# Sums and products with v in four groups of 32 TensorE columns, in a softcapped attention with a gated feed-forward layer

## The chip, the cores and the metric

The kernel runs on one core of one Trainium2 chip. The metric is the device time of one execution in microseconds (us); lower is better. Before the change the median of three runs is 743.75 us (742.98 to 746.29).

## The reference

```python
def _attn_ref(q, k, v, cap):                      # each 8 x 12 x 448 x 64, cap = 30
    scores = scale * np.matmul(q, k.transpose(0, 1, 3, 2))
    scores = cap * np.tanh(scores / cap)
    scores = scores - np.max(scores, axis=-1, keepdims=True)
    attn = np.exp(scores)
    attn = attn / (np.sum(attn, axis=-1, keepdims=True) + 1e-09)
    return np.matmul(attn, v)

def _moe_ref(x, w_val, conv_w, w_out):            # x: 8 x 448 x 768
    ...                                           # gate_pre: causal convolution of x, 5 taps a channel
    gate = 1.0 / (1.0 + np.exp(-gate_pre))
    val = x @ w_val
    return gate * val @ w_out
```

Attention runs over 8 batches and 12 heads; the heads' outputs, side by side, are the x of the second function. All is float32.

## The kernel before, in words

Heads are taken in pairs, six pairs to a batch, 48 pairs in all (`p` from 0 to 47). A tile of 128 partitions holds the 64 dimensions of both heads, one below the other. No maximum is subtracted before the exponent; a small term, `guard`, is added to each sum.

The steps of one pair:

- `load_q`, `load_k`, `load_v` (SyncE's queue, SP) fetch the inputs; `tq`, `tk` (line 305) transpose q and k in blocks of 32 on VectorE (DVE).
- `scores` (L326, TensorE, PE): for each of four groups of 112 keys, both heads at once, keys on partitions and 448 queries along the columns. From pair 13 on (`NPLAIN`) q and k are split in a high and a low part and each product is three matmuls; before that, it is one float32 matmul, which PE makes in two passes.
- `tanh` (L334) and `exp` (L338) on ScalarE (ACT).
- `add` (L345, L348) on DVE: the four groups of keys are added, so that the sums need fewer matmuls: pairs 0 to 5 don't add (four sums steps), pairs 6 to 10 add in twos (two steps), from pair 11 on all four are added (one step).
- `attnv` ("products with v", L363, PE): for each group of keys and each head `j` one matmul with v (112 x 64) as the weights; head 0 writes partitions 0 to 63 of the PSUM tile `psa` (or `psf`), head 1 the partitions 64 to 127. In PE's array these are two groups of 64 columns.
- `sums` (L375, PE): the same with a tile of ones as the weights, so that all 64 partitions of a head hold the sum of each query, in `psz`.
- `turn_sums` (L383, DVE) transposes blocks of 32 x 32 into `zt`: after it, queries lie on partitions. `norm_recip` adds `guard` on the first column of each of the 14 blocks (L389) and takes the reciprocal of these 128 x 14 numbers in one instruction (L390). `spread` (L396) transposes them back, each repeated 32 times. `norm_mul` (L404) multiplies `psa` by the result: `u`, the attention's output.
- `x_hi` (L409, ACT) and `x_lo` (L240, DVE) split u; `conv` (L421, L423, L425) computes the five taps on DVE.

A batch then has the feed-forward part: `sigmoid` (L431, ACT), `val` (L446 to L448, PE, three matmuls for high and low parts), `gate` (L452, DVE), `gated_hi` (L455, ACT), `gated_lo` (L240, DVE), `out_part` (L475 to L477, PE), `store` (L483, ACT) and the output's DMA (L487). The weights are brought from float64 words to two float32r parts in twelve steps during the first dozen pairs (L140 to L150, ACT and DVE).

The order on all engines is written out by hand: each step has a time in units of pairs (`STEADY`, `EARLY`, `PAIRED`, `TOGETHER` and others), all steps are sorted by it, and each engine executes its own in that order, each waiting for what it needs. So a late step holds back what stands behind it on its engine. The tiles `zt` and `rc` exist once.

Of the kernel before, what the change touches and what calls it, by code (L numbers as in the profile page):

```python
# [7 lines left out]
F32 = mybir.dt.float32  # L8
# [5 lines left out]
ALU = mybir.AluOpType  # L14
# [7 lines left out]
P = 128  # L22
ENG = mybir.EngineType

CH = 112
LOAD_ROWS = 112

BLK = 32
# [173 lines left out]
def fast_path(tc, io, u2, q, k, v, w_val, conv_w, w_out, out, capt):  # L202
# [5 lines left out]
    nc = tc.nc  # L208
    B, H, S, D = q.shape
# [4 lines left out]
    NKT = S // CH  # L214
# [6 lines left out]
    PAD = KW - 1  # L221
    GW = TL + S
    ROWS = [slice(j * D, (j + 1) * D) for j in range(2)]

    with ExitStack() as ctx:
        cpool = ctx.enter_context(tc.tile_pool(name="cpool", bufs=1))
        wk = ctx.enter_context(tc.tile_pool(name="wk", bufs=2))
# [18 lines left out]
        guard = cpool.tile([P, 1], F32, name="guard")  # L246
        nc.vector.scalar_tensor_tensor(guard, capt, -1.0, capt, ALU.mult, ALU.min)
        nc.scalar.activation(guard, guard, AF.Exp)
        nc.vector.tensor_scalar_mul(guard, guard, EPS)  # L249
        ones = cpool.tile([P, D], F32, name="ones")  # L250
        nc.gpsimd.memset(ones, 1.0)
        cw = cpool.tile([P, NCC, KW], F32, name="cw")

# [42 lines left out]
        loads, vloads = {(name, 0): t[:, PAD:] for name, t in zip("qk", u2)}, {}  # L296
# [21 lines left out]
        def scores(p, i):  # L318
# [5 lines left out]
            for n, (x, y) in enumerate(parts):  # L324
                for j, r in enumerate(ROWS):
                    nc.tensor.matmul(  # L326
# [23 lines left out]
        def bank(p, name):  # L350

            if p < NEARLY and p % 2:
                return ps_f.tile([P, 512], F32, name="psf")
            return ps_a.tile([P, 512], F32, name=name)

        def attnv(p, i):

            st = state[p]
            if i == 0:
                st["o"] = bank(p, "psa")  # L360
            t = st["p", i]
            for j, r in enumerate(ROWS):
                nc.tensor.matmul(  # L363
                    st["o"][r, :S], vloads[p][:, j, i], t[:, j], start=(i == 0), stop=(i == NKT - 1)
                )

        def sums(p, i):

            st = state[p]
            n = len(tables[p]["sums"])  # L370
            if i == 0:
                st["z"] = bank(p, "psz")
            t = st["p" if n == NKT else "a", i]
            for j, r in enumerate(ROWS):
                nc.tensor.matmul(st["z"][r, :S], ones[:CH], t[:, j], start=(i == 0), stop=(i == n - 1))  # L375
            if i == n - 1:
                vloads.pop(p)

        def turn_sums(p):

            st = state[p]
            st["zt"] = wk.tile([P, S], F32, name="zt", bufs=1)
            nc.vector.transpose(st["zt"], st.pop("z")[:, :S])  # L383

        def norm_recip(p):
            st = state[p]
            rc = wk.tile([P, S // BLK], F32, name="rc", bufs=1)
            col = st["zt"].rearrange("p (c e) -> p c e", e=BLK)[:, :, 0]
            nc.vector.tensor_scalar(rc, col, guard, None, ALU.add)  # L389
            nc.vector.reciprocal(rc, rc)  # L390
            st["rc"] = rc

        def spread(p):
# [116 lines left out]
        def at(when, f, *a):  # L510
# [7 lines left out]
            q_hi=lambda p: half_hi("q", p), k_hi=lambda p: half_hi("k", p),  # L518
            q_lo=lambda p: half_lo("q", p), k_lo=lambda p: half_lo("k", p),
            scores=scores, tanh=tanh, exp=exp, add=add, av=attnv, sums=sums, turn_sums=turn_sums, recip=norm_recip,  # L520
            spread=spread, mul=norm_mul, x_hi=x_hi, x_lo=x_lo, conv=conv,
        )
        for p, table in enumerate(tables):
            for name, f in steps.items():
                x = table.get(name, ())
# [165 lines left out]
def kernel(tc, q, k, v, cap, w_val, conv_w, w_out, out):  # L691
    nc = tc.nc
    with tc.tile_pool(name="cap_pool", bufs=1) as pool, tc.tile_pool(name="io", bufs=2) as io:
        capt = pool.tile([P, 1], F32, name="capt")
        nc.sync.dma_start(capt, cap.rearrange("(o c) -> o c", o=1).partition_broadcast(P))

        pad = conv_w.shape[0] - 1
        u2 = [pool.tile([P, pad + q.shape[2]], F32, name=f"u{i}") for i in range(2)]
        for t, src in zip(u2, (q, k)):
            load_blocks(nc, t[:, pad:], src, 0)  # L700
        mag = pool.tile([1, 1], F32, name="mag")
        nc.vector.scalar_tensor_tensor(mag, capt[0:1], -1.0, capt[0:1], ALU.mult, ALU.max)
        small = pool.tile([1, 1], I32, name="small")
        nc.vector.tensor_scalar(small, mag, CAP_FAST, None, ALU.is_le)
        flag = nc.values_load(small, min_val=0, max_val=1)
        with tc.If(flag != 0) as cmp:
            fast_path(tc, io, u2, q, k, v, w_val, conv_w, w_out, out, capt)
        with cmp.Else():
            general_path(tc, q, k, v, w_val, conv_w, w_out, out, capt)
# [30 lines left out]
```

## Time and profile before

| | |
|---|---|
| median of three runs | 743.75 us (742.98, 743.75, 746.29) |
| profiled execution | span 739.6 us from its first to its last instruction; no other time of it is given |
| PE busy | 717.1 us, 97% |
| DVE busy | 593.0 us, 80% |
| ACT busy | 534.7 us, 72% |
| matmul passes of the products (L363) | 768 |
| matmul passes of the sums (L375) | 284 |
| L383, transpose of the sums | 48 times, 31 us |
| L389 and L390, guard and reciprocal | 48 times each, 11.3 and 11.6 us |
| mean granted TensorE clock | 0.998 |

Rows of the profile name the line, the engine, the operation, the tiles (output <- inputs), the shape, and the count (x); behind the bar stand busy time in us, mean duration of one in ns, and the idle time of the engine just before, with what ended it. In a timeline a row begins with its start and its duration in us, rows of equal kind are merged, and the idle time before it stands in brackets. Rows of a stage have start:end and length, the busy time of PE, PEld (weight loads), DVE, ACT and POOL, the granted clock, and the share of the DMA engines with GB/s. Rows of waits say who waited for whom: us in total, times, and the longest. PEldq is PE's sequencer. Matmul passes overlap, so their durations add up to more than the time they take.

### The profile page before, as it was taken

The numbers are of one execution on the slowest core, as the hardware profiler recorded it, in microseconds if no ns is written. First come the engines' busy times: TensorE is split into PE (matmuls) and PEld (weight loads), VectorE is DVE, ScalarE is ACT, GpSimd is POOL, SyncE is SP. The second block draws the span as 40 slices with busy tenths as digits, with TensorE's granted clock in tenths as the row PEclk, the third lists the DMA queues.
The fourth block names the chain that finished last, engine by engine and source line by source line (L and its number), as shares of the span: only waits on it lengthen the run. The fifth ranks groups of instructions, "written<-read, shape, count | busy, mean of one in ns | idle before, by whom it ended". The sixth has DMA issues, their size and how long they took to land.

```text
span 739.6 us, 10858 instructions
## 1 busy us (share of the span) xinstructions
PE 717.1 (97%) x3972; PEld 488.8 (66%) x3972; DVE 593.0 (80%) x972; ACT 534.7 (72%) x708; POOL 9.0 (1%) x16
## 2 busy tenths in 40 slices
PE   5999999999999999999999999999999999999997
PEld 2333655556767776686677766757766876676997
DVE  2899999888997789988899669988899778997410
ACT  5899977787876678776957679587787659774311
POOL 0000001000000000000000000000000000000000
PEclk9999999999999999999999999999999999999999
DMA  6998867854223332224331333223322333200001
GB/s 109 223 212 209 202 171 154 225 118 80 39 49 80 74 74 38 61 67 88 57 57 47 88 75 65 39 69 74 73 38 61 70 87 57 51 24 33 23 22 68
DMA packets 241820, 63.75 MB, mean 86 GB/s; under 512 B 228448, under 2 KB 235616, under 8 KB 241760
## 3 DMA queue, kind: packets, MB, share of 16 engines
q1 hardware_dynamic: 241760, 62.98, 38.6%
q8 instruction: 33, 0.54, 0.3%
q14 instruction: 27, 0.22, 0.1%
HBM read 51.94 MB, written 11.01 MB: 85 GB/s over the span
## 4 chain that ended last, share of the span: by engine, by line
PE 52%; DVE 21%; ACT 13%; issue 2%; SPq 1%; DMA 0%; DVEq 0%; ACTq 0%
PE pss L326 9%; PE psf L475 8%; PE psf L477 7%; PE psf L476 7%; DVE gate L425 7%; PE psa L363 6%; PE psf L446 4%; PE psf L447 4%; PE psf L448 4%; ACT pt L334 3%; PE psz L375 3%; DVE pa L348 3%; ACT gate L431 3%; ACT pt L338 2%; DVE pa L345 2%
## 5 line engine op out<-in xcount | busy, mean ns | idle before, releaser
L334 ACT ACTIVATE pt<-pss,rc 112x896 f32<-112x896 f32 x192 | 185.1, 1004 | 39.2 <-PE pss L326 39.2
L338 ACT ACTIVATE pt<-pt,capt 112x896 f32<-112x896 f32 x192 | 189.6, 1041 | 0.1
L363 PE MATMUL psa<-pt,vn 112*64 112x448 f32 x720 | 147.7, 546 | 0.0
L425 DVE SCALAR_TENSOR_TENSOR gate<-u,cw,gate 128x448 f32<-128x448 f32 x192 | 130.6, 680 | 5.7
L475 PE MATMUL psf<-wo,g_h 128*128 128x384 f32 x336 | 115.7, 344 | 0.0
L477 PE MATMUL psf<-wo,g_l 128*128 128x384 f32 x336 | 112.6, 335 | 0.0
L476 PE MATMUL psf<-wo,g_h 128*128 128x384 f32 x336 | 112.4, 335 | 0.0
L446 PE MATMUL psf<-xh,wv 128*128 128x448 f32 x288 | 107.5, 373 | 0.1
L448 PE MATMUL psf<-xl,wv 128*128 128x448 f32 x288 | 104.5, 363 | 0.0
L447 PE MATMUL psf<-xh,wv 128*128 128x448 f32 x288 | 104.4, 362 | 0.0
L363 PEld LDWEIGHTS psa<-pt,vn 112*64 112x64 f32 x720 | 47.8, 136 | 81.4 <-issue 69.7
L348 DVE TENSOR_TENSOR pa<-pt 112x896 f32<-112x896 f32 x84 | 91.1, 1085 | 2.8 <-ACT pt L338 2.8
L483 ACT COPY osb<-psf 128x384 f32<-128x384 f32 x56 | 26.6, 475 | 65.3 <-PE psf L477 63.6
L383 DVE STREAM_TRANSPOSE zt<-psz 128x448 f32<-128x448 f32 x45 | 28.8, 640 | 54.2 <-PE psz L375 54.2
L475 PEld LDWEIGHTS psf<-wo,g_h 128*128 128x128 f32 x336 | 63.1, 188 | 12.3 <-issue 11.3
L446 PEld LDWEIGHTS psf<-xh,wv 128*128 128x128 f32 x288 | 54.0, 187 | 20.2 <-issue 5.4
L476 PEld LDWEIGHTS psf<-wo,g_h 128*128 128x128 f32 x336 | 63.1, 188 | 0.0
L477 PEld LDWEIGHTS psf<-wo,g_l 128*128 128x128 f32 x336 | 63.1, 188 | 0.0
L326 PE MATMUL pss<-qt,kt 64*112 64x448 f32 x208 | 49.6, 594 | 12.3 <-DVE guard L249 7.8
L455 ACT CAST g_h<-gate 128x448 fp32r<-128x448 f32 x48 | 26.3, 562 | 47.2 <-DVE gate L452 47.0
L326 PE MATMUL pss<-qh,kh 64*112 64x448 f32 x280 | 58.0, 408 | 0.0
L409 ACT CAST xh<-u 128x448 fp32r<-128x448 f32 x48 | 27.1, 566 | 42.3 <-DVE u L404 42.0
(74 smaller groups left out, 908.6 us busy)
## 6 DMA issues: line engine op xcount, KB each, us to landing
vn<-in_v_dram SPq DMA_DIRECT2D x96, 112.0 KB, 2.6
out_dram<-osb SPq DMA_DIRECT2D x56, 192.0 KB, 1.9
qn<-in_q_dram SPq DMA_DIRECT2D x188, 56.0 KB, 2.5
kn<-in_k_dram SPq DMA_DIRECT2D x188, 56.0 KB, 2.4
w_raw<-in_moe_w_val_dram SPq DMA_DIRECT2D x12, 384.0 KB, 5.1
w_late<-in_moe_w_val_dram SPq DMA_DIRECT2D x12, 384.0 KB, 4.4
w_raw<-in_moe_w_out_dram SPq DMA_DIRECT2D x12, 384.0 KB, 3.8
w_late<-in_moe_w_out_dram SPq DMA_DIRECT2D x12, 384.0 KB, 4.8
```

The source lines that it names most:

```text
L326: nc.tensor.matmul(ps[:CH, j, :S], st[x][r, c], st[y][r], start=(n == 0), stop=(n == len(parts) - 1))
L334: nc.scalar.activation(st["p", i], st.pop(("s", i)), AF.Tanh, scale=rc8[:CH])
L338: nc.scalar.activation(t, t, AF.Exp, scale=capt[:CH])
L348: nc.vector.tensor_tensor(st["a", i], st["p", 2 * i], st["p", 2 * i + 1], op=ALU.add)
L363: nc.tensor.matmul(st["o"][r, :S], vloads[p][:, j, i], t[:, j], start=(i == 0), stop=(i == NKT - 1))
L425: nc.vector.scalar_tensor_tensor(g, u[:, i:i + S], cw[:, hp, i:i + 1], g, ALU.mult, ALU.add)
L446: nc.tensor.matmul(o, w_h, xh, start=(c == 0), stop=False)
L447: nc.tensor.matmul(o, w_l, xh, start=False, stop=False)
L448: nc.tensor.matmul(o, w_h, xl, start=False, stop=(c == NCC - 1))
L475: nc.tensor.matmul(o, g_h[:, d, s], w_h, start=(d == 0), stop=False)
L476: nc.tensor.matmul(o, g_h[:, d, s], w_l, start=False, stop=False)
L477: nc.tensor.matmul(o, g_l[:, d, s], w_h, start=False, stop=(d == NCC - 1))
```

## The change

The products and the sums each go to four groups of 32 columns instead of two of 64. A head's products are two matmuls with 32 dimensions of v each, both over all 448 queries. A head's sums are two matmuls with 32 columns of ones, one over the first 224 queries and the other over the second 224 (`HQ`). So `psz` is 224 columns wide, its transpose L383 is half as wide, and `guard` is added to 7 columns instead of 14, into a new tile `zc`. After that, the sums of the two halves of a head's queries lie on different groups of 32 partitions, while the spread needs both halves on both groups. So the reciprocal is taken in eight pieces of 32 partitions x 7 columns; each reads one group of partitions and writes one half of a row group of `rc`: for the output groups 0, 0, 1, 1, 2, 2, 3, 3 the inputs are groups 0, 1, 0, 1, 2, 3, 2, 3. The spread (L396) and all later steps are as they were, and so is the order of all steps.

```diff
+    GROUPS = [slice(g * BLK, (g + 1) * BLK) for g in range(P // BLK)]
+    HQ = S * BLK // D
+    HC = HQ // BLK
...
-        ones = cpool.tile([P, D], F32, name="ones")
+        ones = cpool.tile([P, BLK], F32, name="ones")
...
-            for j, r in enumerate(ROWS):
+            for g, r in enumerate(GROUPS):
+                j, d = divmod(g * BLK, D)
                 nc.tensor.matmul(
-                    st["o"][r, :S], vloads[p][:, j, i], t[:, j], start=(i == 0), stop=(i == NKT - 1)
+                    st["o"][r, :S], vloads[p][:, j, i, d:d + BLK], t[:, j], start=(i == 0), stop=(i == NKT - 1)
                 )
...
-            for j, r in enumerate(ROWS):
-                nc.tensor.matmul(st["z"][r, :S], ones[:CH], t[:, j], start=(i == 0), stop=(i == n - 1))
+            for g, r in enumerate(GROUPS):
+                j, d = divmod(g * BLK, D)
+                q = slice(HQ * d // BLK, HQ * (d // BLK + 1))
+                nc.tensor.matmul(st["z"][r, :HQ], ones[:CH], t[:, j, q], start=(i == 0), stop=(i == n - 1))
...
-            nc.vector.transpose(st["zt"], st.pop("z")[:, :S])
+            nc.vector.transpose(st["zt"][:, :HQ], st.pop("z")[:, :HQ])
...
-            col = st["zt"].rearrange("p (c e) -> p c e", e=BLK)[:, :, 0]
-            nc.vector.tensor_scalar(rc, col, guard, None, ALU.add)
-            nc.vector.reciprocal(rc, rc)
+            zc = wk.tile([P, HC], F32, name="zc", bufs=1)
+            col = st["zt"].rearrange("p (c e) -> p c e", e=BLK)[:, :HC, 0]
+            nc.vector.tensor_scalar(zc, col, guard, None, ALU.add)
+            for g, r in enumerate(GROUPS):
+                j, d = divmod(g * BLK, D)
+                for x in range(D // BLK):
+                    nc.vector.reciprocal(rc[r, x * HC:(x + 1) * HC], zc[GROUPS[j * D // BLK + x]])
```

## The prediction

> **What bounds the kernel now.** I read the page's totals first, then the busy time by stage, then the waits inside the long stage, and last the timeline of one batch on VectorE (DVE), with the chain beside it.
>
> ```profile
> span 739.6 us, 10858 instructions
> PE 717.1 (97%) x3972; PEld 488.8 (66%) x3972; DVE 593.0 (80%) x972; ACT 534.7 (72%) x708; POOL 9.0 (1%) x16
> ```
>
> ```profile
> 13.00:75.00 62.00, 59.44 (x288) 20.03 (x284) 52.24 (x94) 59.41 (x72) 0.23 (x1) 1.00 0.93 209
> 75.00:174.00 99.00, 95.81 (x477) 58.79 (x474) 90.85 (x147) 79.43 (x102) 3.14 (x2) 1.00 0.68 167
> 174.00:683.00 509.00, 505.13 (x2920) 358.12 (x2920) 433.39 (x701) 378.74 (x507) 5.19 (x6) 1.00 0.30 61
> ```
>
> The totals say TensorE (PE), and the stages (start:end, length, then busy PE, PEld, DVE, ACT) say more. From 13 to 75 us (pairs 0 to 5) ACT is busy 59.41 of 62 us and PE 59.44; from 75 to 174 DVE has 8.15 us of 99 free for some seven pairs, 1.16 us a pair; only from 174 on is PE alone full, and there DVE has 75.6 us free over 35 pairs. But that freedom is not spread evenly:
>
> ```profile
> DVE zt L383 <- PE psz L375: 52.6, 17, 4.9
> PEld psz L375 <- DVE pa L345: 13.1, 12, 1.4
> ```
>
> These are the waits from 174 to 683 us. In 17 pairs DVE stands idle for the sums, 52.6 us in all; in 12 it is the other way round and the sums wait for DVE's additions. One batch (six pairs) on DVE shows why:
>
> ```profile
> 442.48 0.65 DVE L383 STREAM_TRANSPOSE zt<-psz 128x448 f32<-128x448 f32 x1 [2.21 <-PE psz L375]
> ...
> 448.70 1.16 DVE L240 TENSOR_TENSOR g_l<-gate,g_h 128x448 fp32r<-128x448 f32 x2 [0.55 <-ACT g_h L455]
> ...
> 457.84 0.61 DVE L383 STREAM_TRANSPOSE zt<-psz 128x448 f32<-128x448 f32 x1
> ...
> 468.48 0.62 DVE L240 TENSOR_TENSOR g_l<-gate,g_h 128x448 fp32r<-128x448 f32 x1 [0.17 <-ACT g_h L455]
> ...
> 472.31 0.65 DVE L383 STREAM_TRANSPOSE zt<-psz 128x448 f32<-128x448 f32 x1
> 472.99 0.24 DVE L389 TENSOR_SCALAR rc<-zt,guard 128x14 f32<-128x14 f32 x1
> 473.27 0.24 DVE L390 RECIPROCAL rc<-rc 128x14 f32<-128x14 f32 x1
> 473.54 0.65 DVE L396 STREAM_TRANSPOSE zt<-rc 128x448 f32<-128x448 f32 x1
> ...
> 484.09 1.09 DVE L345 TENSOR_TENSOR pa<-pa,pa 112x896 f32<-112x896 f32 x1
> ...
> 499.45 0.65 DVE L383 STREAM_TRANSPOSE zt<-psz 128x448 f32<-128x448 f32 x1 [1.74 <-PE psz L375]
> ```
>
> ```profile
> 485.24 0.97 PE psz L375 x4
> ```
>
> From 442.48 to the addition that ends at 485.18 DVE goes almost without a break (it holds three normalizations, at 442.48, 457.84 and 472.31), and the sums of 485.24 start when that addition is done: this run of 43 us is DVE's, with PE at most a microsecond behind. From 485.24 to the next run the sums come last (DVE waits 1.74 us at 499.45). The 12 waits of PE are two to a run, so there are six such runs. What a change to PE and DVE is worth must be read separately in the two kinds of stretch.
>
> **The change part by part.**
>
> *Products with v, four groups of 32 columns.* Twice the matmuls, each still streaming all 448 queries.
>
> ```profile
> 408.51 3.23 PE L363 MATMUL psa<-pt,vn 112*64 112x448 f32 x16
> 411.57 0.92 PE L375 MATMUL psz<-pa,ones 112*64 112x448 f32 x4
> 412.42 0.46 PE L326 MATMUL pss<-qh,kh 64*112 64x448 f32 x2
> ```
>
> Sixteen matmul passes start within 3.06 us (408.51 to 411.57), 0.191 each although one lasts 0.54: the two column groups run side by side, and a slot of two passes is 3.06/8 = 0.38 us. With four groups side by side the eight slots stay as they are: 0. The upper bound is two and two, eight more slots, +3.1 us a pair; nothing here can gain, since each group streams as many queries as before. I take 0, because the row shows that groups are not served in turn.
>
> *Sums, 224 queries a group.* Four passes in 412.42 - 411.57 = 0.85 us now, two slots and the change to the next shape. A slot of 224 columns is 0.19, so a pair with one sums step saves 0.375 us (37 pairs), with two 0.75 (pairs 6 to 10), with four 1.5 (pairs 0 to 5). The other bound is 0, if instructions come too slowly to fill a slot half as long. What the trace has on that are two waits of PE's sequencer around 16 passes (products and sums of pair 0):
>
> ```profile
> L363 PEldq EVENT_SEMAPHORE  x1: 51/51/51, 13.4 to 13.4; - x1
> ```
> ```profile
> L326 PEldq EVENT_SEMAPHORE  x1: 51/51/51, 14.2 to 14.2; - x1
> ```
>
> 0.8 us for 16 passes with their weight loads is 0.05 a pass; a slot of four needs 0.20, about what it lasts, and the queue ahead of it is full of longer ones. I take the full saving. [...]
>
> *Transpose of the sums (L383), half as wide.* The price per column from two shapes of one operation:
>
> ```profile
> L348 DVE TENSOR_TENSOR pa<-pt 112x896 f32<-112x896 f32 x84 | 91.1, 1085 | 2.8 <-ACT pt L338 2.8
> L404 DVE TENSOR_TENSOR u<-psa,zt 128x448 f32<-128x448 f32 x45 | 28.1, 624 | 1.5
> ```
>
> 448 columns more cost 0.461 us, so 224 fewer save 0.23. The addition of the guard on 7 columns instead of 14 saves nothing worth counting.
>
> *Eight reciprocals for one.* No row shows an instruction on 32 partitions, nor one whose partitions begin elsewhere than its predecessor's. The nearest:
>
> ```profile
> L390 DVE RECIPROCAL rc<-rc 128x14 f32<-128x14 f32 x48 | 11.6, 242 | 1.7
> ```
> ```profile
> 4.51 0.17 DVE L243 RECIPROCAL rc<-capt 128x1 f32<-128x1 f32 x1 [0.75 <-DVE small L704]
> 4.59 0.14 DVE L247 SCALAR_TENSOR_TENSOR guard<-capt 128x1 f32<-128x1 f32 x1
> ```
> ```profile
> 18.23 0.18 DVE L148 TENSOR_SCALAR cw_m<-cw_m 128x30 int32<-128x30 int32 x1
> 18.35 0.18 DVE L149 TENSOR_SCALAR cw_t<-cw 128x30 int32<-128x30 int32 x1
> ```
>
> From 1 to 14 columns a reciprocal goes from 0.17 to 0.242, 6 ns a column, so one of 7 lasts about 0.20 (estimate). If each waits for the one before, as L390 does in its place (473.27 to 473.54, 0.03 behind the end), a piece costs 0.235 and eight 1.88. If they overlap as the small ones of 4.51 and 18.23 do (0.08 and 0.12 from start to start), eight last 0.8 to 1.07 with the tail. Against the 0.275 now that is +1.60, or +0.5 to +0.8. I take the row nearest in operation and place, L390: +1.60. Upper end: no shorter at 7 columns, 8 x 0.276, +1.93.
>
> [...]
>
> Together VectorE has +1.60 - 0.23 = **+1.36 us a pair** (d below), between the same two instructions: behind them stand the spread, the product u that ACT's xh waits for, and all later additions and transposes on DVE's queue.
>
> *Pairs 0 to 5.* Here PE's saving is worth nothing, because ACT is as full as PE; and DVE is as full as both:
>
> ```profile
> 33.54 0.65 DVE L383 STREAM_TRANSPOSE zt<-psf 128x448 f32<-128x448 f32 x1 [0.97 <-PE psf L375]
> ```
> ```profile
> 55.94 0.62 DVE L404 TENSOR_TENSOR u<-psf,zt 128x448 f32<-128x448 f32 x1
> ```
> ```profile
> 56.59 0.56 ACT L409 CAST xh<-u 128x448 fp32r<-128x448 f32 x1
> ```
> ```profile
> 64.29 0.64 DVE L383 STREAM_TRANSPOSE zt<-psz 128x448 f32<-128x448 f32 x1
> ```
>
> After 33.54 DVE waits for nobody (three pairs to 64.29, 10.25 us each), and ACT starts xh 0.03 us after u is done. So d goes straight into the period: the first pair hides 0.97 of it at 33.54 (+0.4), four more add 1.36 each, less 0.2 of slips: +5.6.
>
> *75 to 174 us.* Seven pairs at 1.36 - 1.16 = 0.2 if every gap of DVE can be used, 1.4 us; some gaps move along with ACT, so I take +2.
>
> *The six runs.* At the first normalization the sums end 0.375 earlier and DVE adds 1.36; 0.53 vanishes in the wait of 0.55 at 448.70. The next two add 1.36 each, 0.17 vanishes at 468.48. The addition at the run's end is 3 x 1.36 - 0.375 - 0.53 - 0.17 = 3.0 us later, so the two waits of PE grow by what PE saved and by this. In the three pairs after it PE sets the pace and saves 3 x 0.375 = 1.1, as long as DVE's slack lasts (1.74 - 0.375 - 1.36 = 0.0 at 499.45, just). A run: +1.9. Six: +11.4, and 0.4 more since the last run has only two such pairs behind it: +11.8.
>
> *The end.* After 683 us PE works on alone; the last sums save 0.4.
>
> ```profile
> 683.00:740.00 57.00, 51.50 (x281) 49.83 (x279) 13.32 (x23) 12.74 (x24) 0.00 (x0) 0.97 0.10 36
> ```
>
> Sum: 5.6 + 2 + 11.8 - 0.4 = **+19 us**. The profiled execution spans 739.6 us, so 758.6; the median of the three runs, 743.75, lies 4.15 above that span, which start and end around it account for and which does not change: **763 us**, slower by 2.6%. With a piece at 0.20 and no gap d is 1.12 and the sum +12; at 0.276 d is 1.70 and the sum +31, with DVE's slack at 499.45 overdrawn. The forecast's own range is 755 to 775.
>
> **Rivals.**
>
> *The pieces overlap; not slower.* Starts 0.12 apart give d = +0.57: pairs 0 to 5 cost 2.3, 75 to 174 us gains about 1 from the shorter sums, a run costs 2 x 0.57 - 0.17 = 1.0 and gives back 1.1: 744. Starts 0.08 apart, d = +0.29: 739. It turns at about 0.11 us from start to start. For it speak the rows at 4.51 and 18.23, against it that those pairs all begin at partition 0.
>
> *The four groups do not run side by side.* Then 48 pairs pay 3.1 us on PE and the sums gain nothing: +145, less the 5 us in which PE now stands waiting for additions: some 880. Against it speaks the two-by-two overlap at 408.51; that it goes on to four no row shows.
>
> *The sums do not get shorter*, for want of instructions. Then a run keeps +1.36 - 0.55 + 2 x 1.36 - 0.17 = 3.4 and gives nothing back: 6 x 3.4 + 7.6 = +28, 772. Against it the 0.05 us a pass.
>
> **Chances.** Forecast 0.69; overlap 0.18 (0.12 within 0.5%, 0.06 below); groups in turn 0.06; no shorter sums 0.07. Half a percent (3.7 us) is about what a measurement of this kernel can tell from no change. Slower 0.82, within 0.12, faster 0.06. The range 741 to 777 holds the forecast, the shorter-sums rival and most of the overlap case, and leaves out groups in turn and the best of the overlap.
>
> **What would show it.** The products' eight slots still take 3.1 us, now with 32 passes; the sums' slots are 0.19 apart with four passes each; L383 lasts 0.41 us; the eight reciprocals start about 0.235 apart (right) or 0.08 to 0.12 (wrong); DVE is busy some 60 us more; PE's idle time from 174 to 683 us, 3.9 us now, grows to some 30, at the sums or where it waits for DVE's last results of a run; in pairs 0 to 5 the period goes from 10.25 to 11.6 us. The forecast fails if the reciprocals start closer than about 0.11 us, or if DVE's additional time falls into its 52.6 us of waiting for sums rather than into the runs.

## The result, and the profile after

The changed kernel takes 770.33 us (median; 769.78 to 770.80) and the kernel before, in the same measurement, 745.02 (742.98 to 746.30): a ratio of 1.0353, 95% interval 1.0326 to 1.0380, so slower by 25.3 us. 763 was forecast, with a range of 741 to 777. The four runs of the changed kernel had a mean granted clock of 0.986 to 0.988, the later runs of the kernel before 0.992 to 1.000. Below, *before* and *after* stand for the two kernels.

The page's totals of the changed kernel:

```profile
span 768.0 us, 13298 instructions
PE 706.7 (92%) x5024; PEld 481.4 (63%) x5024; DVE 642.6 (84%) x1308; ACT 537.4 (70%) x708; POOL 9.0 (1%) x16
```

PE is busy 10.4 us less than before and DVE 49.6 us more. By stage, with the border at 683 us moved to 715 because the kernel is late there (start:end, length, busy PE, PEld, DVE, ACT, POOL, then the granted clock, DMA share, GB/s):

```profile
13.00:75.00 62.00, 48.66 (x438) 18.61 (x436) 52.10 (x121) 53.79 (x66) 0.23 (x1) 0.94 0.86 203
75.00:174.00 99.00, 88.51 (x572) 51.48 (x570) 90.16 (x177) 74.11 (x94) 3.17 (x2) 0.95 0.64 158
174.00:715.00 541.00, 516.19 (x3751) 363.63 (x3748) 486.05 (x983) 392.45 (x522) 5.19 (x6) 1.00 0.29 60
```

PE, which stood idle for 3.9 us in the long stage, now stands idle for 541 - 516.19 = 24.8. What ended that idle time, from the list of waits between 174 and 715 us (total, times, longest), with DVE's own wait below it:

```profile
PE psf L485 <- ACT g_h L465: 7.8, 6, 1.4
PE psz L381 <- DVE pa L348: 7.1, 7, 1.3
PE psf L456 <- DVE gate L462: 6.8, 6, 1.2
PE psf L485 <- ACT osb L493: 2.9, 6, 0.6
...
DVE zt L389 <- PE psz L381: 29.8, 15, 4.0
```

Three kinds of wait come once in each of the six runs of DVE (that for the additions seven times), 3.6 us a run together: for the additions, as before, and now also for the gate (DVE) and for g_h (ACT, behind that gate). The fourth, ACT's copies of osb, was not in the prediction. DVE's own wait for the sums fell from 52.6 to 29.8 us.

The changed groups, and PE on one pair (start, duration):

```profile
L400 DVE RECIPROCAL rc<-zc 32x7 f32<-32x7 f32 x384 | 73.8, 192 | 6.7
...
L381 PE MATMUL psz<-pa,ones 112*32 112x224 f32 x376 | 25.7, 355 | 7.1 <-DVE pa L348 7.1
L389 DVE STREAM_TRANSPOSE zt<-psz 128x224 f32<-128x224 f32 x45 | 18.0, 400 | 32.2 <-PE psz L381 32.2
```
```profile
429.17 3.21 PE L367 MATMUL psa<-pt,vn 112*32 112x448 f32 x32
432.20 0.56 PE L381 MATMUL psz<-pa,ones 112*32 112x224 f32 x8
432.69 0.46 PE L329 MATMUL pss<-qh,kh 64*112 64x448 f32 x2
```

The products need 432.20 - 429.17 = 3.03 us for 32 passes, 3.06 before for 16. The sums need 0.49 for eight, 0.85 before for four. And the same batch on DVE as in the prediction, 20 us later:

```profile
462.76 0.42 DVE L389 STREAM_TRANSPOSE zt<-psz 128x224 f32<-128x224 f32 x1 [0.78 <-PE psz L381]
463.21 0.23 DVE L396 TENSOR_SCALAR zc<-zt,guard 128x7 f32<-128x7 f32 x1
463.48 1.63 DVE L400 RECIPROCAL rc<-zc 32x7 f32<-32x7 f32 x8
465.14 0.65 DVE L406 STREAM_TRANSPOSE zt<-rc 128x448 f32<-128x448 f32 x1
...
478.83 0.38 DVE L389 STREAM_TRANSPOSE zt<-psz 128x224 f32<-128x224 f32 x1
...
494.36 0.41 DVE L389 STREAM_TRANSPOSE zt<-psz 128x224 f32<-128x224 f32 x1
...
507.28 1.09 DVE L348 TENSOR_TENSOR pa<-pa,pa 112x896 f32<-112x896 f32 x1
...
521.88 0.42 DVE L389 STREAM_TRANSPOSE zt<-psz 128x224 f32<-128x224 f32 x1
```

Eight reciprocals last 1.63 us, (1.63 - 0.192)/7 = 0.205 from start to start, so each starts 0.013 behind the end of the one before. The wait of 1.74 us before the fifth transpose (499.45 then, 521.88 now) is gone.

Where the time came from is read best from one event a pair, the start of the transpose of the sums (zt), as kernel minus before, in us. The kernels of the experiments are beside it:

| pair | before at | after | pieces alone | no pieces | one and four | from pair 12 | store first | where it waits | both |
|---|---|---|---|---|---|---|---|---|---|
| 0 | 22.24 | -0.1 | -0.4 | -0.5 | -0.4 | -0.2 | -0.6 | 0.0 | 0.1 |
| 1 | 33.54 | 1.2 | 0.0 | -0.3 | -0.3 | 4.0 | 1.4 | 0.9 | 2.9 |
| 5 | 74.82 | 5.5 | 5.2 | 1.3 | 1.9 | 3.8 | 5.7 | 1.2 | 2.8 |
| 8 | 123.56 | 8.8 | 9.2 | 0.6 | 3.7 | 3.9 | 9.1 | 1.2 | 2.8 |
| 9 | 136.50 | 11.8 | 12.9 | 1.2 | 6.4 | 3.9 | 11.9 | 4.2 | 5.5 |
| 12 | 179.55 | 12.7 | 14.9 | -0.6 | 6.2 | 4.0 | 12.9 | 4.0 | 5.2 |
| 18 | 269.16 | 15.7 | 20.3 | -2.1 | 6.6 | 6.9 | 14.4 | 3.2 | 4.0 |
| 24 | 352.94 | 17.2 | 24.0 | -3.6 | 6.6 | 8.3 | 15.9 | 2.1 | 2.8 |
| 30 | 442.48 | 20.3 | 29.4 | -5.0 | 7.1 | 11.3 | 17.8 | 1.3 | 1.6 |
| 36 | 526.26 | 21.8 | 33.0 | -6.5 | 7.1 | 12.7 | 19.4 | 0.2 | 0.4 |
| 42 | 615.88 | 24.8 | 38.4 | -8.1 | 7.4 | 15.6 | 21.5 | -0.7 | -0.8 |
| 47 | 682.79 | 28.5 | 43.8 | -8.9 | 8.8 | 19.4 | 25.2 | -0.8 | -1.2 |

So the 28.5 us between the two spans are 5.5 by pair 5, 7.2 more by pair 12, and 15.7 from there on. Steps of some 3 us at pair 1 or between pairs 8 and 9 also stand in kernels that have no pieces there (from pair 12, where it waits, both); the last section says what stands behind them.

### The profile page after: what moved, and what is told of

The parts are those of the page before. It is cut to its first block, busy times and chain, and to the rows that moved or that the text cites. A ratio compares the mean times of both kernels' runs of the same rounds, so it can differ in the third digit from the quotient of the medians.

```text
span 768.0 us, 13298 instructions
## 1 busy us (share of the span) xinstructions
PE 706.7 (92%) x5024; PEld 481.4 (63%) x5024; DVE 642.6 (84%) x1308; ACT 537.4 (70%) x708; POOL 9.0 (1%) x16
## 4 chain that ended last, share of the span: by engine, by line
PE 35%; DVE 35%; issue 5%; ACT 4%; DMA 1%; DVEq 0%; SPq 0%; ACTq 0%
PE psa L367 7%; DVE gate L435 6%; PE pss L329 6%; PE psf L485 5%; DVE rc L400 5%; PE psf L487 5%; PE psf L486 5%; DVE pa L351 4%; DVE zt L406 2%; DVE gate L462 2%; PE psf L456 2%; DVE u L414 2%; PE psf L457 2%; PE psf L458 2%; DVE g_l L243 2%
## 5 line engine op out<-in xcount | busy, mean ns | idle before, releaser
L367 PE MATMUL psa<-pt,vn 112*32 112x448 f32 x1440 | 149.5, 551 | 0.0
L485 PE MATMUL psf<-wo,g_h 128*128 128x384 f32 x336 | 117.0, 348 | 10.7 <-ACT g_h L465 7.8
L456 PE MATMUL psf<-xh,wv 128*128 128x448 f32 x288 | 109.0, 379 | 7.1 <-DVE gate L462 6.8
L457 PE MATMUL psf<-xh,wv 128*128 128x448 f32 x288 | 105.8, 367 | 0.0
L367 PEld LDWEIGHTS psa<-pt,vn 112*32 112x32 f32 x1440 | 42.6, 111 | 85.8 <-issue 69.0
L329 PE MATMUL pss<-qt,kt 64*112 64x448 f32 x208 | 52.3, 618 | 30.4 <-ACT pt L337 22.6
L400 DVE RECIPROCAL rc<-zc 32x7 f32<-32x7 f32 x384 | 73.8, 192 | 6.7
L485 PEld LDWEIGHTS psf<-wo,g_h 128*128 128x128 f32 x336 | 63.0, 187 | 25.4 <-issue 10.5
```

Of the source, the lines that this page charges most:

```text
L329: nc.tensor.matmul(ps[:CH, j, :S], st[x][r, c], st[y][r], start=(n == 0), stop=(n == len(parts) - 1))
L367: nc.tensor.matmul(st["o"][r, :S], vloads[p][:, j, i, d:d + BLK], t[:, j], start=(i == 0), stop=(i == NKT - 1))
L456: nc.tensor.matmul(o, w_h, xh, start=(c == 0), stop=False)
L457: nc.tensor.matmul(o, w_l, xh, start=False, stop=False)
L485: nc.tensor.matmul(o, g_h[:, d, s], w_h, start=(d == 0), stop=False)
```

## The experiments

The theory: the pieces on DVE are held, which means that each starts only when the one before it has ended (0.013 us behind it in the changed kernel); they are the loss, and what PE saves is only taken where PE sets the pace. Rivals: the 32-column groups, the clock or the val matmuls cost the time; or small instructions cost 0.2 us each however they are placed.

**The pieces alone** (the kernel before, with this edit):

```diff
-            nc.vector.tensor_scalar(rc, col, guard, None, ALU.add)
-            nc.vector.reciprocal(rc, rc)
+            zc = wk.tile([P, S // BLK], F32, name="zc", bufs=1)
+            nc.vector.tensor_scalar(zc, col, guard, None, ALU.add)
+            for g in range(4):
+                r = slice(g * 32, g * 32 + 32)
+                for x in range(2):
+                    o, c = g // 2 * 2 + x, slice(x * 7, x * 7 + 7)
+                    nc.vector.reciprocal(rc[r, c], zc[o * 32:o * 32 + 32, c])
```

> The kernel before with eight reciprocals of 32x7 on the same partitions as in the change, and nothing else of it. Theory (the pieces are held one behind the other, and this alone is the loss): starts 0.20 us apart, the block from first reciprocal to spread 1.67 us instead of 0.275, so d = +1.39 a pair with no saving on TensorE or on the transpose to set against it. Pairs 0 to 5: +1.39 x 4.8 = +6.6; pairs 6 to 12 about +8; each run +2 to +4.2. 745 + 35 = 780, at least 770. Rival (32-column groups, a lower clock or slower val matmuls cost the time, the pieces little): below 757. Val matmuls should start every 200 ns as before.

786.4 us, ratio 1.0576 (1.0542 to 1.0610): +42, more than the whole change and 6 more than I expected. The pieces alone lose more than the change does; the rest of the change gives some 16 us of it back. The val matmuls did not stay at 200 ns: 203.7, for which see the shifted tile below.

**No pieces** (the changed kernel, with this edit):

```diff
-            for g, r in enumerate(GROUPS):
-                j, d = divmod(g * BLK, D)
-                for x in range(D // BLK):
-                    nc.vector.reciprocal(rc[r, x * HC:(x + 1) * HC], zc[GROUPS[j * D // BLK + x]])
+            halves = zc.unsqueeze(1).to_broadcast([P, D // BLK, HC])
+            nc.vector.reciprocal(rc.rearrange("p (x c) -> p x c", c=HC), halves)
```

> The changed kernel with one reciprocal of 128x14 that reads its 7 columns twice; it leaves out the exchange between the two halves of the queries, so that half of the queries are divided by other queries' sums. Theory: without the pieces d is -0.24 a pair and the savings of TensorE remain: each run -0.24 x 3 - 0.375, and -1.1 in the three pairs behind it, together some -13, 75 to 174 us -1, the val matmuls at 205 ns give back 2 to 4: 732 (726 to 740), faster than before. Rival (groups, clock or val matmuls cost the time): above 745. The granted clock should not fall to 0.5 before the end.

This kernel leaves out the exchange between the two halves of the queries, so it shows a time and not a way to get it. 733.23 us, ratio 0.9854 (0.9822 to 0.9886): faster by 11, as expected. From pair 12 on each batch of six gains 1.5 us. The rivals that blame groups or val matmuls fall with it, since both are in this kernel. The clock did fall here, to 0.50 near 23 and 132 us, against what I wrote, so the clock alone is not the loss either.

**Pieces that are not held** (before, with the 14 columns in eight pieces on all partitions):

```diff
-            nc.vector.reciprocal(rc, rc)
+            for x in range(8):
+                c = slice(x * 7 // 4, (x + 1) * 7 // 4)
+                nc.vector.reciprocal(rc[:, c], zc[:, c])
```

> The kernel before with eight reciprocals for one that all take 128 partitions from partition 0, each on one or two of the 14 columns (it differs from the pieces-alone kernel in the partitions, not in the count). Theory (what costs is the hold between pieces that begin on other partitions): they start 0.08 to 0.12 us apart, d = +0.3 to +0.8, and the time is 752 to 764, less than half the loss of the pieces-alone kernel. Rival (it is the count: every small instruction takes its 0.2 us): starts 0.18 to 0.21 apart and the same time as the pieces-alone kernel.

750.85 us, ratio 1.0093 (1.0061 to 1.0125), just below my range. DVE's timeline of the pieces alone, then of this kernel:

```profile
410.03 1.63 DVE L395 RECIPROCAL rc<-zc 32x7 f32<-32x7 f32 x8
411.70 0.65 DVE L401 STREAM_TRANSPOSE zt<-rc 128x448 f32<-128x448 f32 x1
```
```profile
404.26 0.59 DVE L393 RECIPROCAL rc<-zc 128x1 f32<-128x1 f32 x8
404.89 0.65 DVE L399 STREAM_TRANSPOSE zt<-rc 128x448 f32<-128x448 f32 x1
```

The same count of eight, and 1.67 us from the first reciprocal to the spread becomes 0.63. With 0.148 for one piece on average they start (0.59 - 0.148)/7 = 0.063 apart. So the cost is not that there are eight. What sets the held pieces apart is that each begins on another group of partitions than the one before; they also have 32 partitions and 7 columns where these have 128 and one or two. The columns are an unlikely cause, since the instructions of 30 columns at 18.23 us of the kernel before start 0.12 apart; pieces of 32 partitions that all begin on the same group are in no run. Measured is 0.205 from start to start for 32 partitions with changing groups and 0.063 for all 128 partitions; that it is the change of group that holds a piece is my reading, which no run parts from the number of partitions.

**The groups alone** (after, with sums over all queries and one transpose and reciprocal):

```diff
-                nc.tensor.matmul(st["z"][r, :HQ], ones[:CH], t[:, j, q], start=(i == 0), stop=(i == n - 1))
+                nc.tensor.matmul(st["z"][r, :S], ones[:CH], t[:, j], start=(i == 0), stop=(i == n - 1))
```

> The changed kernel with four groups of 32 columns for products and sums, but each sums group over all 448 queries, and the one transpose and one reciprocal of the kernel before. Theory (32-column groups run side by side and cost nothing): the time of before, 745 within 3 us. Rival (twice the matmuls and weight loads cost TensorE time): 750 or more, with slots over 0.38 us.

744.89 us beside 744.27, ratio 1.0019 (1.0001 to 1.0036): at most 0.4%, where the rival had 750 or more. Its profile is 5.5 us late by pair 9, in two steps of some 3 us at pairs 1 and 9 that other kernels have too, and from pair 12 to 47 this goes from 5.3 to 4.8: there the four groups cost nothing.

**A shifted tile, both ways.** The val matmuls of the changed kernel are slower without a change to them. After, with zc twice as wide, and before, with an unused tile:

```diff
-            zc = wk.tile([P, HC], F32, name="zc", bufs=1)
+            zc = wk.tile([P, 2 * HC], F32, name="zc", bufs=1)[:, :HC]
```

> The changed kernel with its new 28-byte tile (zc) made 56 bytes wide, so that all tiles laid out behind it move by 32 bytes; no instruction changes. Theory (the val matmuls became slower because xh and xl lie at other addresses): val matmuls start every 200.4 ns again instead of 205.3, TensorE is busy 4.2 us less, time -1 to -4. Rival (they are slower through the clock or through weight loads of the new groups): still 205 ns and no change.

```diff
+            pad = wk.tile([P, 7], F32, name="pad", bufs=1)
+            nc.vector.memset(pad, 0.0) if p == 0 else None
             col = st["zt"].rearrange("p (c e) -> p c e", e=BLK)[:, :, 0]
```

> The kernel before with an unused tile of 28 bytes laid out ahead of xh and xl (and one small memset to it at the first pair). Theory: val matmuls start every 205.3 ns instead of 200.4, 864 x 4.9 ns = 4.2 us more on TensorE, most of it on the path: +2 to +4.5. Rival: 200.4 ns and no change.

The third of the three val matmuls in the groups of before, of after, of after with the wider zc, of before with the unused tile:

```profile
L448 PE MATMUL psf<-xl,wv 128*128 128x448 f32 x288 | 104.5, 363 | 0.0
```
```profile
L458 PE MATMUL psf<-xl,wv 128*128 128x448 f32 x288 | 105.9, 368 | 0.0
```
```profile
L458 PE MATMUL psf<-xl,wv 128*128 128x448 f32 x288 | 105.4, 366 | 0.0
```
```profile
L450 PE MATMUL psf<-xl,wv 128*128 128x448 f32 x288 | 105.9, 368 | 0.0
```

From start to start that is 200.4, 205.3, 203.7 and 205.4 ns. The unused tile alone makes them slow: 744.97 us, ratio 1.0027 (1.0011 to 1.0042), some 2 us, as expected. The wider zc did not bring 200.4 back and not a shorter time (771.4 us, ratio 1.0375, 1.0353 to 1.0396): my expectation was wrong in that any shift by 32 bytes would undo it, and the changed kernel does not gain from 1.4 us of PE time in any case. By the layout that the program gives the tiles, xh begins 32 bytes behind a multiple of 128 in the kernels at 200 ns (before, groups alone, and the later ones that lay out zc behind xh), 64 behind in those at 205 (after, no pieces, unused tile), and 96 behind in those at 203.7 (wider zc, pieces alone, not held, one and four). Why, no run shows.

**One and four** (after with the wider zc; one reciprocal over both halves, then the four that cross):

```diff
+            halves = zc.unsqueeze(1).to_broadcast([P, D // BLK, HC])
+            nc.vector.reciprocal(rc.rearrange("p (x c) -> p x c", c=HC), halves)
             for g, r in enumerate(GROUPS):
-                j, d = divmod(g * BLK, D)
-                for x in range(D // BLK):
-                    nc.vector.reciprocal(rc[r, x * HC:(x + 1) * HC], zc[GROUPS[j * D // BLK + x]])
+                x = 1 - g % 2
+                nc.vector.reciprocal(rc[r, x * HC:(x + 1) * HC], zc[GROUPS[g ^ 1]])
```

> The changed kernel, padded as above, with one reciprocal over 128 partitions that writes both halves and four pieces of 32x7 that then replace the halves that come from the other group: five instructions for eight. Theory: one of 0.24 and four of 0.205, 1.06 us for the 1.67 of eight, so d = +0.55 for +1.15; the loss of 25 falls by more than half, 752 to 758, less the padding's 1 to 4: 748 to 757. Rival (the pieces' length hardly matters, it is groups or clock): within 5 us of the changed kernel.

```profile
404.93 0.24 DVE L398 RECIPROCAL rc<-zc 128x14 f32<-128x14 f32 x1
405.21 0.81 DVE L401 RECIPROCAL rc<-zc 32x7 f32<-32x7 f32 x4
406.05 0.65 DVE L407 STREAM_TRANSPOSE zt<-rc 128x448 f32<-128x448 f32 x1
```

750.54 us, ratio 1.0094 (1.0067 to 1.0121), as expected. From the first reciprocal to the spread it takes 1.12 us instead of 1.67, so d, what DVE has more to do in a pair, is 1.12 - 0.28 - 0.24 = +0.60. In the table the batches 18 to 24 and 30 to 36 now cost nothing: what a run loses, the three pairs behind it return.

**From pair 12 on** (after, with `if half(p)` around sums, transpose and reciprocal, half(p) being p >= 12; the others as in the groups alone).

> The changed kernel with half-query sums and pieces from pair 12 on only; pairs 0 to 11 have four groups over all queries, one transpose and one reciprocal. zc is then laid out behind xh and xl. Theory: the changed kernel's transposes of the sums come 12.7 us late by pair 12; this part goes, 770.3 - 12.7 = 757.6, less 1 to 4 if the val matmuls run at 200 ns: 753 to 758. The granted clock does not fall to 0.5 before 174 us. Rival (the lateness of the first pairs is made up later anyway): 765 or more.

760.72 us, ratio 1.0225 (1.0198 to 1.0252), 3 to 8 above the expectation. In its table column nothing is added between pairs 1 and 12, and from 12 to 47 it loses 15.4, as the changed kernel does (15.7): the two stretches are separate. The expected time was too low by about the 4.0 us that this profile holds at pair 1 and the kernel before doesn't: PE waits 3.22 us for vn at 26.85, where the kernel before waits 1.18 at 25.06, and the granted clock is 0.57 from 27 to 31 us, which I had ruled out. Whether the other three executions lost the same there isn't shown.

**Only where DVE waits.** half(p) is p >= 12 and p % 6 >= 3, first with five instructions and zc as in one and four, then with all eight pieces:

> Four groups everywhere, but half-query sums, with one reciprocal and four pieces, only in the last three pairs of each batch of six from pair 12 on, where VectorE waits for the sums (18 pairs); all other pairs have sums over all queries, one transpose and one reciprocal. Theory (what counts is whose stretch a pair lies in): TensorE saves 0.375 us in each of these pairs, d = +0.6 falls into VectorE's wait of 1.74 us: 18 x 0.375 = 6.7 less, 735 to 738.5 against 742 to 744. Rival (a piece costs its time wherever it stands): 18 x 0.6 less 6.7 = +4, 746 or more.

> As the kernel that waits (half-query sums only in the last three pairs of a batch), but with the eight pieces of the change. d = +1.15 a pair just fits into the wait of 1.74 us less the 0.375 that the sums come earlier. Theory: TensorE's saving remains, less what slips past the wait of the first of the three: 736 to 741, faster than before though each of the 18 pairs has all eight held pieces. Rival (a piece costs its time wherever it stands): 18 x 1.15 less 6.7 = +14, 756.

Five: 740.75 us beside 743.16, ratio 0.9963 (0.9943 to 0.9983), faster but not by what I expected. Ten of its twelve runs had a clock of 0.991 to 0.995; the two at 0.997 and 0.999 took 737.75 and 737.51, within what I expected, where the nine runs of before at 0.998 or more took 740.80 to 743.16. Whether this kernel makes the clock fall more often no run settles. Eight: 744.25, ratio 1.0018 (0.9998 to 1.0037), a miss; but the 18 x 1.15 = 20.7 us of additional DVE work cost nothing on balance, where the rival had 756. DVE before the sixth transpose of the batch that the prediction shows, in before and with five:

```profile
512.61 0.65 DVE L383 STREAM_TRANSPOSE zt<-psz 128x448 f32<-128x448 f32 x1 [1.71 <-PE psz L375]
```
```profile
512.79 0.42 DVE L396 STREAM_TRANSPOSE zt<-psz 128x224 f32<-128x224 f32 x1 [0.73 <-PE psz L382]
```

It still waits for the sums, 0.73 us of the 1.71: the additional 0.60 and the sums' 0.36 came out of the wait. With five, batches with six out tiles gain 1.1 us (3.1 to 2.1 from pair 21 to 24), the full 3 x 0.36, but those with eight gain 0.7; with eight pieces 1.1, and -0.4. Between pairs 46 and 47, at the end, 0.64 comes back with five and 1.27 with eight: about d, since no later pair has room for it.

**Store first** (the changed kernel, with this edit):

```diff
-                at(t0 + y + 0.20, store, b, m)
+                at(t0 + y + (0.08 if b % 2 and y in (10.36, 11.36) else 0.20), store, b, m)
```

> The changed kernel with one thing moved: in the batches whose out matmuls are eight a batch, ACT copies the first two finished out tiles (osb) ahead of xh and not behind it. Theory (in these batches TensorE waits for a psf bank because the copy stands behind xh, which waits for VectorE's late u): the stalls of 0.62 us at 422.87 and 0.5 us at 439.4 go, the loss from pair 12 to 18, 24 to 30 and 36 to 42 falls from 3.0 to about 1.9, and the time by 3 to 4: 766.5 to 767.5. Rival (the copy only ends last; TensorE would have waited for something else at once): within 1 us of 770.

The stall in the changed kernel, on ACT and PE:

```profile
420.01 0.57 ACT L419 CAST xh<-u 128x448 fp32r<-128x448 f32 x1 [0.81 <-DVE u L414]
420.49 1.97 ACT L341 ACTIVATE pt<-pt,capt 112x896 f32<-112x896 f32 x2
422.37 0.45 ACT L493 COPY osb<-psf 128x384 f32<-128x384 f32 x1
```
```profile
422.87 0.44 PE L485 MATMUL psf<-wo,g_h 128*128 128x384 f32 x1 [0.62 <-ACT osb L493]
```

PE needs the bank of an out tile that ACT hasn't copied yet, because ACT stands at xh, and xh at DVE's late u. PE's waits from 174 to 715 us with the copy ahead of xh:

```profile
PE psf L485 <- ACT g_h L465: 7.8, 6, 1.4
PE psf L456 <- DVE gate L462: 6.8, 6, 1.2
PE psz L381 <- DVE pa L348: 4.3, 4, 1.3
PE psf L456 <- ACT osb L493: 0.3, 1, 0.3
```

767.21 us, ratio 1.0325 (1.0299 to 1.0351), as expected, though this interval overlaps that of the changed kernel (1.0326 to 1.0380) and the waits show the gain more surely than the time: the six waits for osb at L485 are gone, three of those for pa with them, and the batches of pairs 12, 24 and 36 lose 1.5, 2.0 and 2.1 instead of 3.0. In the last two of these batches this execution had its clock at half for 3.4 us, at 409 and 586 us, so they may lose less without that.

**Both** (where it waits with five, store first, pairs 46 and 47 as before).

> The kernel that waits, with five instructions (half-query sums in the last three pairs of a batch), with the copies of osb moved ahead of xh as in the store-first kernel, and with pairs 46 and 47 left at sums over all queries. In the kernel that waits, a batch with six out tiles gained 1.1 us and one with eight 0.75, and 0.64 came back between pairs 46 and 47. Theory: the batches with eight gain the 0.33 that they lacked, three times, and some 0.3 at the end: 1.3 less than the kernel that waits, 0.994 of before. Rival (osb ahead of xh holds up ACT where u is not late): no better than the kernel that waits, 0.996 or more.

738.59 us beside 743.62, ratio 0.9927 (0.9899 to 0.9955): faster than both kernels, by 5 us against before. The batches with eight out tiles now gain 1.1 like the others, and nothing comes back at the end.

## Why the prediction was right, and where its steps failed

The prediction was right in sign and in what costs the time. That 763 came within 7.3 us of 770.33 is partly luck: two terms of the sum were too small, and the 4.15 us added to the span were 2.4 too many, which made up for a part. By its steps:

- *Products, 0.* Right: 3.03 us for 3.06, and the groups alone at 1.0019.
- *Sums, 0.375 saved a pair.* Right: 0.85 - 0.49 = 0.36, and 1.1 us for three pairs in the kernels where DVE had room. The rival without shorter sums is out, and so is that of groups in turn.
- *Eight reciprocals, +1.60.* The right row, and each piece did start behind the end of the one before; the gap was too large: between held pieces it is 0.013 us, not the 0.035 behind an instruction that waits for a result. 1.67 - 0.28 = +1.39 was measured, d = +1.15 for +1.36. The rival of overlapping pieces is out; the kernel whose pieces are not held shows what it would have looked like.
- *Pairs 0 to 5, +5.6.* 5.5 by the table, but two errors cancel: 1.15 a pair for 1.36, and at pair 1 nothing was hidden, where I had 0.97, because the clock was down from 23 to 30 us (0.51). The kernel with the wider zc, without that drop, is 4.0 late by pair 5.
- *75 to 174 us, +2.* The step that failed most: 7.2. I let DVE's gaps of 8.15 us take the additional work. Up to pair 8 they took none: 1.1 us a pair, which is d: DVE is idle for 3.17 us between 75 and 123.6 us before, and still for 3.47 in the same pairs after, 80 to 132.4. Most of these gaps are waits for ACT (2.3 us in before, 2.4 in after), and they moved along with DVE; that ACT is late because DVE is, I infer. Only from pair 10 on is some absorbed (13.0, 13.3, 12.7 us late at 10, 11 and 12). Of the 2.9 us from pair 8 to 9, I put the 1.8 beyond one d down to a lower clock (0.51 from 139 to 146 us, below).
- *The six runs, +11.8 with the end.* 15.7. Batches with six out tiles lost 1.5 (1.9 forecast, with the larger d). The waits of 0.55 and 0.17 us in a run went, as forecast; two more for g_h that the sum passes over, 0.63 each at 466.60 and 478.08 in before, stayed in the changed kernel, so the run had more breaks than I saw. Those with eight lost 3.0: a term was missing, the copies of osb behind xh. Store first showed 0.9 to 1.5 of it. The sum had the pairs behind a run gain as long as DVE's own slack lasts, and didn't ask who stands behind ACT's wait for u. In the last batch, 1.27 returned between pairs 46 and 47, where I had 0.4.
- *The val matmuls.* Not seen at all: 864 x 4.9 ns = 4.2 us on PE from a tile of 28 bytes. On a kernel bound by PE it cost some 2 us; the changed kernel with the wider zc, 1.4 us cheaper on PE, was not faster.
- *4.15 us from the span to the time.* Wrong: the profiled execution of after took 769.78 us for its span of 768.0, 1.8 more, and the other kernels' are alike. For the other 2.4 the clock is the likely cause: the three runs have none on record, but later runs of before at 0.998 or more took 740.6 to 743.6 us, those at 0.996 or less 742.2 to 746.3. This made the forecast in us 2.4 higher and hid part of the low sum: +19 against 28.5 between the spans, +25.3 between the medians.

## What to carry to other kernels

Eight reciprocals of 32 x 7, each on another group of 32 partitions than the one before, took 0.205 us each here, 0.013 more than one lasts, where eight on all 128 partitions took 0.063 each. So splitting one small instruction for the sake of another engine can be paid in full on DVE; do it only in the stretches where the trace shows DVE waiting for that engine (here five instructions gained there and eight did not), and count from which pair on no slack is left. An engine's free time in a stage is slack only if what ends it doesn't move along: look at who ends each gap. And behind a late result ask what stands on the queue of the engine that waits for it, here a copy that freed a PSUM bank.

## What the runs showed of the hardware that was not expected

**The clock fell in kernels that left the place as it was.** Granted clock (the number before the DMA share) in after, in before with the unused tile, and in before:

```profile
23.00:30.00 7.00, 5.74 (x32) 2.82 (x34) 6.77 (x18) 6.03 (x9) 0.00 (x0) 0.51 0.94 201
108.00:112.00 4.00, 3.93 (x20) 1.03 (x24) 3.49 (x6) 3.97 (x6) 0.00 (x0) 0.57 0.00 0
139.00:146.00 7.00, 5.38 (x26) 1.44 (x28) 6.71 (x10) 7.00 (x9) 0.00 (x0) 0.51 0.63 168
```
```profile
130.00:137.00 7.00, 6.37 (x18) 1.99 (x20) 5.59 (x9) 7.00 (x9) 0.00 (x0) 0.52 0.65 206
```
```profile
130.00:137.00 7.00, 6.22 (x31) 2.53 (x32) 6.30 (x10) 7.00 (x9) 0.00 (x0) 1.00 0.69 209
```

In the last two, PE waits twice for ACT's pt just ahead of 131 us, 0.97 and 1.62 us with the unused tile, 1.45 and 1.61 in before. The execution with the unused tile then had half its clock for some 7 us and came 3 us later to pair 9; that of before, with no less idle time, did not. After has one stretch of 3.44 us of waiting ahead of the drop at 139; with the unused tile none is longer than 1.62, and in store first the clock halved behind single waits of 1.33, 1.22 and 1.31 us. So the clock fell behind waits shorter than the 1.61 us behind which it stayed at 1.00 in before. What decides is open. Thirteen runs of before spread from 740.59 us (granted clock 0.998) to 745.18 (0.995). A step of 3 us at pair 9 therefore says nothing of a change. One at pair 1 has a load in front of it: vn's load was issued at 23.13, 23.83 and 24.14 us in groups alone, both and from pair 12, at 21.96 in before, PE stood idle for 2.74, 2.36 and 3.22 us instead of 1.18, and the clock was at half for 3.4 us about the end of that wait. Why the load was late, no run shows.

**The address of the moving operand.** Val matmuls of 128x448 start every 200.4, 203.7 or 205.3 ns according to where xh and xl lie (32, 96 or 64 bytes behind a multiple of 128). The scores, whose operands moved by the same bytes in the three kernels named here, changed by some 1 ns: a slot is 220.8, 222.0 or 221.2 ns in before, pieces alone and the changed kernel. The out matmuls took 173 to 174 ns everywhere, but their operands lie at the same place in all kernels, so they say nothing on this.
